# Seven half-size products for eight in the output product of a gated MoE block

## The chip, the cores and the metric

The kernel runs on one core of a Trainium2 chip. The metric is the device time of one execution in microseconds (us), as the median of several executions. Times of one experiment and of the kernel before were taken on the same chip in the same session.

## The reference

```python
# q, k, v: (B=8, H=8, S=576, D=64); w_gate, w_val: (512, 1536); w_out: (1536, 512); w_res: (512, 512)
kv  = einsum('bhsd,bhse->bhde', k, v)
o   = einsum('bhsd,bhde->bhse', q, kv)
x   = o / sqrt(mean(o*o, -1) + 1e-6) * g_norm          # then (B*S, H*D) = (4608, 512)
ffn = (gelu(x @ w_gate) * (x @ w_val)) @ w_out
out = x + sigmoid(x @ w_res) * ffn                       # 4608 x 512, float32
```

## The kernel before

All matmuls take fp16 tiles, and their sums are kept in fp32 tiles. The 4608 tokens are worked in nine blocks of 512. Blocks 0 to 7 hold the first 512 tokens of each batch entry, and block 8 holds the 8 x 64 tokens left over (the remainder). A block has twelve slots for the up-projections (gate and value, one 128-wide piece of F = 1536 per slot) and then four tiles of 128 tokens, each with a residual gate and an output product. The attention of the next block is worked between these slots, on whatever engine has room.

```python
pmoe  = ctx.enter_context(tc.tile_pool(name="pmoe", bufs=4, space=bass.MemoryType.PSUM))
pattn = ctx.enter_context(tc.tile_pool(name="pattn", bufs=4, space=bass.MemoryType.PSUM))
# ... cut ...
def m_act(blk, f, gps, vps):                      # hid = gelu(gate) * value
    ge = moep.tile([P, NJ * P], FP16, tag="ge", name="ge")
    nc.scalar.activation(out=ge, in_=gps, func=AF.Gelu)
    nc.vector.tensor_tensor(out=hids[blk][:, f, :], in0=ge, in1=vps, op=ALU.mult)

def m_res(blk, j):                                # residual gate: four matmuls, then tanh on ACT
    rps = pmoe.tile([P, C], FP32, tag="mm", name="rps")
    # ... cut ...
    nc.scalar.activation(out=th, in_=rps, func=AF.Tanh, scale=0.5)
    return th

def m_out(blk, j):                                # 12 output matmuls of 512 columns per tile
    # ... cut ...
    th = m_res(blk, j)
    fps = pmoe.tile([P, C], FP32, tag="mm", name="fps")
    for f in range(NF):
        m_ffn(blk, j, f, fps)
    m_store(blk, j, m_gate(th, fps))              # (th + 1) * fps, then 0.5 * that + t, on DVE
```

The attention of block 1 ends inside block 0's output product. Its normalisation is a chain of twelve small operations on VectorE (DVE). The scaled result `t` is then transposed on TensorE (PE).

```python
def a_norm(b, j0, j1):                            # 1/sqrt by Newton, on 128x32 or 128x40 elements
    # ... cut ...
    nc.vector.tensor_scalar(out=m, in0=ss, scalar1=1.0 / D, scalar2=RMS_EPS, op0=ALU.mult, op1=ALU.add)
    # ... cut: two more tensor_scalar ...
    for _ in range(3):
        nc.vector.tensor_tensor(out=a, in0=yy, in1=yy, op=ALU.mult)
        nc.vector.tensor_tensor(out=a, in0=a, in1=mh, op=ALU.mult)
        nc.vector.scalar_tensor_tensor(out=yy, in0=a, scalar=1.5, in1=yy, op0=ALU.add, op1=ALU.mult)

# attention of block 1, by slots of block 0
NF + 6: [lambda: a_norm(b, 0, NJ), t[0], t[1], t[2], t[3]],
2 * NF: [x[0], x[1]],                             # x[j]: transposes of tile j on PE
2 * NF + 1: [x[2]],
2 * NF + 2: [x[3]],
```

## Time and profile before

| | before |
|---|---|
| median of 3 executions | 350.04 us (349.79 to 350.08) |
| span in the profile | 348.1 us, mean granted clock 1.000 |
| PE, PE weight loads, DVE busy | 97%, 46%, 61% |
| ACT (ScalarE), POOL (GpSimd) busy | 35%, 14% |

The lines that bound the reading are in the prediction below. Some hints for them:

- In views by order of time, a line gives the start, the time taken, the engine and the line of the program, then output<-inputs, their shapes and the count. An idle time ahead of the group and what ended it stand in square brackets.
- Matmuls overlap in the pipeline, so the pace of a group is read from its start to the start of the next group, not from its duration: in the kernel before a 128x512 matmul has a mean duration of 379 ns, while twelve of them start within 2.59 us, 0.216 each.
- The row of PE clocks gives the granted clock in forty slices of the span. 9 is full speed, 5 about half.

Two more facts of the kernel before are needed later. The first is the first operation of block 1's normalisation, in DVE's order of time:

```profile
48.62 0.18 DVE L249 TENSOR_SCALAR nm<-ss 128x32 f32<-128x32 f32 x1
```

The second is what PE does at that point, in its order of time:

```profile
52.50 0.62 PE L284 MATMUL xtp<-ident,t 128*128 128x128 f16 x8
52.95 1.03 PE L364 MATMUL fps<-wo,hid 128*128 128x512 f16 x4
...
56.07 1.02 PE L331 MATMUL gps<-xT,wg 128*128 128x512 f16 x4
```

The norm operation takes 0.18 us. PE reaches the transposes of its result at 52.50 without a wait, and is through with them and the last output matmuls at 56.07, in 3.57 us.

### The profile page before, as it was taken

The page shows a single profiled execution, that of the slowest core. Times are in us where ns is not written, and L with a number is a line of the kernel's source. Part 1 is how long each engine was busy: PE and PEld are TensorE (multiplying, and loading weights), DVE is VectorE, ACT ScalarE, POOL GpSimd, SP SyncE. Part 2 cuts the span into 40 slices and gives each one's busy share as a digit, 9 for nine tenths or more (in the row PEclk, how much of TensorE's full clock was granted, in tenths as well). Part 3 has the DMA queues.
Part 4 walks back from the last instruction along what each step waited for, and adds up shares of the span by engine and source line. Part 5 has one row for each costly group of instructions (what it writes and reads, how often), then busy time and mean ns, then how long its engine had stood idle before and what let it go on. Part 6 is the DMA issues. An engine that isn't in the chain of part 4 may idle for free.

```text
span 348.1 us, 5543 instructions
## 1 busy us (share of the span) xinstructions
PE 338.4 (97%) x2162; PEld 159.5 (46%) x2162; DVE 211.9 (61%) x432; ACT 122.0 (35%) x212; POOL 50.2 (14%) x79
## 2 busy tenths in 40 slices
PE   8699999999999999999999999999999999999995
PEld 3444544444444444444444444444444444444443
DVE  6755377769748765766478656855686444344433
ACT  3663544362254213421353125312732233223320
POOL 2782420150050005000320031000000000000000
PEclk9999999999999999999999999999999999999999
DMA  7999999697889078904792569045002500020013
GB/s 240 311 206 202 196 202 136 173 148 93 190 142 118 0 175 157 132 0 123 141 184 16 135 140 185 5 101 157 0 2 56 140 2 0 30 91 2 0 30 92
DMA packets 78508, 38.77 MB, mean 111 GB/s; under 512 B 42386, under 2 KB 74002, under 8 KB 78482
## 3 DMA queue, kind: packets, MB, share of 16 engines
q0 software_dynamic: 38752, 17.17, 38.9%
q1 hardware_dynamic: 39488, 21.11, 23.0%
q8 instruction: 17, 0.28, 0.3%
q10 hardware_dynamic: 242, 0.13, 0.1%
q14 instruction: 9, 0.07, 0.1%
HBM read 38.80 MB, written 9.44 MB: 139 GB/s over the span
## 4 chain that ended last, share of the span: by engine, by line
PE 92%; DMA 4%; DVE 2%; SPq 0%; issue 0%; POOL 0%; ACT 0%; DVEq 0%
PE gps L331 27%; PE fps L364 26%; PE vps L331 26%; PE rps L351 9%; DMA vf<-in_v_dram 2%; DMA kf<-in_k_dram 1%; PE kvp L182 1%; PE op L200 1%; DMA qrT<-qr 1%; DVE t L601 1%; DVE ss L587 1%; PE vps L627 0%; PE fps L394 0%; PE gps L627 0%; PE xtp L284 0%; PE orp L228 0%
## 5 line engine op out<-in xcount | busy, mean ns | idle before, releaser
L320 DVE TENSOR_TENSOR hid<-ge,vps 128x512 f16<-128x512 f16 x108 | 73.4, 685 | 68.4 <-PE vps L331 66.3
L331 PE MATMUL gps<-xT,wg 128*128 128x512 f16 x424 | 109.0, 379 | 0.0
L331 PE MATMUL vps<-xT,wv 128*128 128x512 f16 x424 | 108.8, 379 | 0.0
L319 ACT ACTIVATE ge<-gps 128x512 f16<-128x512 f32 x108 | 64.3, 597 | 118.6 <-PE gps L331 106.6
L364 PE MATMUL fps<-wo,hid 128*128 128x512 f16 x420 | 96.5, 379 | 0.0
L331 PEld LDWEIGHTS <-wv 128*128 128x128 f16 x424 | 41.5, 98 | 50.0
L364 PEld LDWEIGHTS <-hid 128*128 128x128 f16 x420 | 40.8, 98 | 48.5
L331 PEld LDWEIGHTS <-wg 128*128 128x128 f16 x424 | 40.2, 98 | 46.8 <-issue 0.2
L370 DVE SCALAR_TENSOR_TENSOR pf<-th,fps 128x512 f32<-128x512 f32 x35 | 23.8, 687 | 48.1 <-PE fps L364 48.1
L360 ACT ACTIVATE th<-rps 128x512 f32<-128x512 f32 x36 | 21.5, 598 | 79.5 <-PE rps L351 79.5
L351 PE MATMUL rps<-wr,xT 128*128 128x512 f16 x144 | 36.5, 379 | 0.0
L375 DVE SCALAR_TENSOR_TENSOR osb<-pf,t 128x512 f32<-128x512 f32 x35 | 24.2, 691 | 1.1
L219 DVE TENSOR_REDUCE ss<-sq 128x8 f32<-128x512 f32 x32 | 20.6, 679 | 2.9 <-ACT sq L217 2.7
L351 PEld LDWEIGHTS <-xT 128*128 128x128 f16 x144 | 14.1, 98 | 17.0
L733 POOL COPY hold<-qT 1x1 f16<-1x1 f16 x5 | 0.9, 178 | 133.8 <-DMA qT<-q 133.8
L277 DVE TENSOR_TENSOR t<-op,ny 128x512 f16<-128x512 f32 x28 | 17.9, 682 | 0.1
L217 ACT ACTIVATE sq<-op 128x512 f32<-128x512 f32 x28 | 15.3, 597 | 4.5 <-PE op L200 4.2
L291 DVE TENSOR_TENSOR t<-t,g 128x512 f16<-128x512 f16 x36 | 13.3, 418 | 0.0
L512 PE MATMUL idle<-zeros 128*128 128x512 f16 x19 | 7.2, 505 | 1.2 <-DVE zeros L485 1.2
L99 POOL DMA_DIRECT2D qraw<-in_q_dram x7 | 6.3, 895 | 5.9 <-DVE q L107 4.0
L101 POOL DMA_DIRECT2D v<-in_v_dram x7 | 6.3, 904 | 0.0
L100 POOL DMA_DIRECT2D kraw<-in_k_dram x7 | 6.3, 899 | 0.1
(102 smaller groups left out, 166.0 us busy)
## 6 DMA issues: line engine op xcount, KB each, us to landing
out_dram<-osb SPq DMA_DIRECT2D x32, 256.0 KB, 2.4
qraw<-in_q_dram POOLq DMA_DIRECT2D x7, 512.0 KB, 6.1
kraw<-in_k_dram POOLq DMA_DIRECT2D x7, 512.0 KB, 8.5
v<-in_v_dram POOLq DMA_DIRECT2D x7, 512.0 KB, 11.0
wg<-in_moe_w_gate_dram POOLq DMA_DIRECT2D x2, 512.0 KB, 8.8
wv<-in_moe_w_val_dram POOLq DMA_DIRECT2D x2, 512.0 KB, 9.5
wo<-in_moe_w_out_dram POOLq DMA_DIRECT2D x2, 512.0 KB, 13.6
out_dram<-osb SPq DMA_DIRECT2D x6, 128.0 KB, 2.3
```

Source lines behind the costliest of these rows:

```text
L217: nc.scalar.activation(out=sq, in_=src, func=AF.Square)
L219: nc.vector.tensor_reduce(out=out_, in_=sq, op=ALU.add, axis=mybir.AxisListType.X)
L277: nc.vector.tensor_tensor(out=t, in0=o, in1=scale, op=ALU.mult)
L291: nc.vector.tensor_tensor(out=t_t[blk][:, jj, :], in0=t_t[blk][:, jj, :], in1=g16, op=ALU.mult)
L319: nc.scalar.activation(out=ge, in_=gps, func=AF.Gelu)
L320: nc.vector.tensor_tensor(out=hids[blk][:, f, :], in0=ge, in1=vps, op=ALU.mult)
L331: nc.tensor.matmul(ps[:, j0 * P : j1 * P], lhsT=w[:, cc, :], rhs=xT_t[blk][:, j0:j1, cc, :], start=(cc == 0 and j0 == 0), stop=(cc == NP - ...
L351: nc.tensor.matmul(rps, lhsT=xT_t[blk][:, j, cc, :], rhs=wr16[:, cc, :], start=(cc == 0), stop=(cc == NP - 1),)
L360: nc.scalar.activation(out=th, in_=rps, func=AF.Tanh, scale=0.5)
L364: nc.tensor.matmul(fps, lhsT=hids[blk][:, f, j * P : (j + 1) * P], rhs=wo16[:, f, :], start=(f == 0), stop=(f == NF - 1))
L370: nc.vector.scalar_tensor_tensor(out=pf, in0=th, scalar=1.0, in1=fps, op0=ALU.add, op1=ALU.mult)
L375: nc.vector.scalar_tensor_tensor(out=osb, in0=pf, scalar=0.5, in1=t_t[blk][:, j, :], op0=ALU.mult, op1=ALU.add)
```

## The change

The intent is to stream fewer columns through PE. The output product of a block is (512 x 1536)·(1536 x 512). Cut both factors into 2 x 2 parts A and B: tokens, the 1536 and the 512 columns are each halved. Strassen's scheme in Winograd's form needs seven half products where the plain way needs eight:

- Sums of the weights, once per kernel on POOL: t0 = B12−B11, t1 = B22−t0, t2 = B22−B12, t3 = B21−t1.
- Sums of the hidden activations, once per block on DVE: s0 = A21+A22, s1 = s0−A11, s2 = A11−A21, s3 = A12−s1.
- Products, each of 2 x 6 matmuls of 256 columns. PSUM banks go on summing from what another engine put into them (E from ACT's copy, F from DVE's sum, in seven blocks, so 14 times per execution): A = A11·B11, E ← A (copied by ACT), D = s0·t0, d ← D (copied by ACT), A += s1·t1, F ← A+d (DVE), E += A12·B21, A += s2·t2, c22 = A+d (DVE), F += s3·B22, A += A22·t3. The four results are E, F, A and c22.

The matmul count of the output product rises from 48 to 84 per block, while its columns fall by one eighth. To find SBUF for the sums, the hidden tiles go from two buffers to one and the result tiles are shared. The residual gate's tiles move to the attention's PSUM pool. Blocks 0 and 8 keep the plain product. The core of the diff:

```diff
-    hidp = ctx.enter_context(tc.tile_pool(name="hidp", bufs=2))
+    hidp = ctx.enter_context(tc.tile_pool(name="hidp", bufs=1))
@@ cut @@
+    def wo_sums(i):
+        pairs = [(b_of(1, 2), b_of(1, 1)), (b_of(2, 2), wo_t[:, 0]), (b_of(2, 2), b_of(1, 2)), (b_of(2, 1), wo_t[:, 1])]
+        for f in range(0, NFH, 2):
+            sub(nc.gpsimd, wo_t[:, i, f : f + 2, :], *(x[:, f : f + 2, :] for x in pairs[i]))
+    def s_begin(blk):
+        s_ = hid_sums
+        sub(nc.vector, s_[2], a_of(blk, 1, 1), a_of(blk, 2, 1))
+    def s_rest(blk):
+        s_ = hid_sums
+        sub(nc.vector, s_[0], a_of(blk, 2, 1), a_of(blk, 2, 2), ALU.add)
+        sub(nc.vector, s_[1], s_[0], a_of(blk, 1, 1))
+        sub(nc.vector, s_[3], a_of(blk, 1, 2), s_[1])
@@ cut @@
+                m_res(blk, j, pattn, "at")
@@ cut @@
+            prod(w["A"], a_of(blk, 1, 1), b_of(1, 1), True)
+            nc.scalar.copy(out=w["E"], in_=w["A"])
+            prod(w["D"], s_[0], wo_t[:, 0], True)
+            nc.scalar.copy(out=w["d"], in_=w["D"])
@@ cut @@
+            prod(w["A"], s_[1], wo_t[:, 1], False)
+            sub(nc.vector, w["F"], w["A"], w["d"], ALU.add)
+            prod(w["E"], a_of(blk, 1, 2), b_of(2, 1), False)
+            pf((0, 0), w["E"])
+            prod(w["A"], s_[2], wo_t[:, 2], False)
@@ cut: c22, F's and A's last products, gating and stores @@
-            2 * NF + 2: [x[3]],
+            2 * NF + 2: [x[3], lambda: [wo_sums(i) for i in range(4)]],
@@ cut @@
-            k0, o0, n0 = 4, 6, 10
+            k0, o0, n0 = 5, 7, 10
         else:
-            at(m - 1, NF + 1, lambda: by_token(b, "q"))
-            at(m - 1, NF + 2, *begin)
+            at(m - 1, NF - 2, lambda: by_token(b, "q"))
+            at(m - 1, NF + 1, *begin)
@@ cut @@
+                plan.setdefault(NFH + 2, []).insert(0, lambda: s_begin(blk))
+                plan.setdefault(NF - 1, []).append(lambda: (s_rest(blk), outs.extend(out_by_products(blk))))
```

More of the change, by code (lines that the diff above doesn't have):

```diff
@@ L117 @@
     wr16 = wpool.tile([P, NP, C], FP16, name="wr16")
+    wo_ts = wpool.tile([P, NF * C], FP16, name="wo_ts")
+    hid_s = wpool.tile([P, NF * NJ * P], FP16, name="hid_s")
+    th_all = finp.tile([P, NJ, C], FP32, bufs=1, name="th")
+    res_all = finp.tile([P, NJ, C], FP32, bufs=1, name="osb")
     def load_columns(dst, src, i):
@@ L346, in m_gval, with m_res @@
         m_act(blk, f, gps, vps)
-    def m_res(blk, j):
-        rps = pmoe.tile([P, C], FP32, tag="mm", name="rps")
+    def m_res(blk, j, pool=pmoe, tag="mm"):
+        rps = pool.tile([P, C], FP32, tag=tag, name="rps")
         for cc in range(NP):
@@ L357, in m_res @@
             )
-        th = finp.tile([P, C], FP32, tag="th", bufs=NJ, name="th")
+        th = th_all[:, j, :]
         nc.scalar.activation(out=th, in_=rps, func=AF.Tanh, scale=0.5)
@@ L366, in m_ffn, with m_gate @@
         )
-    def m_gate(th, fps):
-        pf = finp.tile([P, C], FP32, tag="pf", bufs=NJ, name="pf")
+    def m_gate(j, th, fps):
+        pf = res_all[:, j, :]
         nc.vector.scalar_tensor_tensor(out=pf, in0=th, scalar=1.0, in1=fps, op0=ALU.add, op1=ALU.mult)
@@ L373, in m_store @@
     def m_store(blk, j, pf):
-        osb = finp.tile([P, C], FP32, tag="osb", bufs=3, name="osb")
+        osb = pf
         nc.vector.scalar_tensor_tensor(
@@ L388, in m_out_last @@
         th = m_res(blk, j)
-        osb_all = finp.tile([P, C], FP32, tag="osb", bufs=3, name="osb")
         for c0, n in ((0, C // 2), (C // 2, C // 4), (3 * C // 4, C // 4)):
@@ L400, in m_out_last @@
                 )
-            pf = finp.tile([P, n], FP32, tag="pf", bufs=NJ, name="pf")
+            osb = pf = res_all[:, j, cs]
             nc.vector.scalar_tensor_tensor(out=pf, in0=th[:, cs], scalar=1.0, in1=fps, op0=ALU.add, op1=ALU.mult)
-            osb = osb_all[:, cs]
             nc.vector.scalar_tensor_tensor(
@@ L417, in m_out, with b_of, a_of @@
             m_ffn(blk, j, f, fps)
-        m_store(blk, j, m_gate(th, fps))
+        m_store(blk, j, m_gate(j, th, fps))
+    NFH, CH, PR = NF // 2, C // 2, M0 // 2
+    wo_t = wo_ts.rearrange("p (i f c) -> p i f c", i=4, f=NFH)
+    hid_sums = hid_s.rearrange("p (i f t) -> p i f t", i=4, f=NFH)
+    hid_sums = [hid_sums[:, i] for i in range(4)]
+    def b_of(i, j):
+        return wo16[:, (i - 1) * NFH : i * NFH, (j - 1) * CH : j * CH]
+    def a_of(blk, i, j):
+        return hids[blk][:, (j - 1) * NFH : j * NFH, (i - 1) * PR : i * PR]
@@ new lines, in sub @@
+    def sub(eng, out_, in0, in1, op=ALU.subtract):
+        eng.tensor_tensor(out=out_, in0=in0, in1=in1, op=op)
+    def wo_sums(i):
[10 more added lines that the diff above has]
+        sub(nc.vector, s_[3], a_of(blk, 1, 2), s_[1])
@@ new lines, in prod, with out_by_products, res, first_two @@
+    def prod(ps, a, b, start):
+        for e in range(2):
+            for f in range(NFH):
+                nc.tensor.matmul(
+                    ps[:, e, :],
+                    lhsT=a[:, f, e * P : (e + 1) * P],
+                    rhs=b[:, f, :],
+                    start=(start and e == 0 and f == 0),
+                    stop=(f == NFH - 1),
+                    skip_group_check=True,
+                )
+    def out_by_products(blk):
+        w = {}
+        s_ = hid_sums
+        def res(jj):
+            for j in (2 * jj, 2 * jj + 1):
+                m_res(blk, j, pattn, "at")
+        def first_two():
+            for n in ("D", "E", "F", "A"):
+                w[n] = pmoe.tile([P, 2, CH], FP32, tag="mm", name="w" + n)
+            w["d"] = finp.tile([P, 2, CH], FP32, tag="wd", bufs=1, name="wd")
+            prod(w["A"], a_of(blk, 1, 1), b_of(1, 1), True)
+            nc.scalar.copy(out=w["E"], in_=w["A"])
+            prod(w["D"], s_[0], wo_t[:, 0], True)
+            nc.scalar.copy(out=w["d"], in_=w["D"])
+        def part(jj):
+            return slice(None), slice(2 * jj[0], 2 * jj[0] + 2), slice(jj[1] * CH, (jj[1] + 1) * CH)
+        def pf(jj, src):
+            nc.vector.scalar_tensor_tensor(
+                out=res_all[part(jj)], in0=th_all[part(jj)], scalar=1.0, in1=src, op0=ALU.add, op1=ALU.mult
+            )
+        def fin(jj):
+            of = part(jj)
+            nc.vector.scalar_tensor_tensor(
+                out=res_all[of], in0=res_all[of], scalar=0.5, in1=t_t[blk][of], op0=ALU.mult, op1=ALU.add
+            )
+        def store(jj):
+            dst = out[blk * S : blk * S + M0, :].rearrange("(p j) c -> p j c", j=NJ)
+            js = slice(2 * jj, 2 * jj + 2)
+            nc.sync.dma_start(out=dst[:, js, :], in_=res_all[:, js, :])
+        def others():
+            prod(w["A"], s_[1], wo_t[:, 1], False)
[3 more added lines that the diff above has]
+            prod(w["A"], s_[2], wo_t[:, 2], False)
+            c22 = res_all[part((1, 1))]
+            sub(nc.vector, c22, w["A"], w["d"], ALU.add)
+            prod(w["F"], s_[3], b_of(2, 2), False)
+            pf((0, 1), w["F"])
+            fin((0, 0))
+            prod(w["A"], a_of(blk, 2, 2), wo_t[:, 3], False)
+            pf((1, 1), c22)
+            pf((1, 0), w["A"])
+            fin((0, 1))
+            store(0)
+            fin((1, 1))
+            fin((1, 0))
+            store(1)
+        return [lambda: res(0), lambda: res(1), first_two, others]
@@ L430, in step @@
             if f == NF - 1:
-                pfs.extend(m_gate(ths[j], fpss[j]) for j in range(NJ))
+                pfs.extend(m_gate(j, ths[j], fpss[j]) for j in range(NJ))
         slots += [lambda f=f: step(f) for f in range(NF)]
@@ L437 @@
     tiles_16(0)
-    raw[0, "q"] = stage.tile([P, H, NJ * D], FP32, name="qf")
+    raw[0, "q"] = wo_ts.bitcast(FP32)[:, 0 : H * NJ * D].rearrange("p (h x) -> p h x", h=H)
     hid_of = {}
     for which in "kv":
-        t = hidp.tile([P, NF, NJ * P], FP16, tag="hid", name=which + "f")
-        hid_of[which] = t = t.rearrange("p a b -> p (a b)")
+        if which == "k":
+            t = hidp.tile([P, NF, NJ * P], FP16, tag="hid", name=which + "f").rearrange("p a b -> p (a b)")
+        else:
+            t = hid_s
+        hid_of[which] = t
         raw[0, which] = t.bitcast(FP32)[:, 0 : H * NJ * D].rearrange("p (h x) -> p h x", h=H)
@@ L452 @@
         first_last.append(t[:, 2 * H * NJ * D :][:, 0 : 2 * H * D].rearrange("p (j h d) -> p j h d", j=2, h=H))
-        first_raw.append([finp.tile([P, C], FP32, tag="th", bufs=NJ, name=f"{which}l") for _ in range(2)])
+        first_raw.append([th_all[:, 2 * len(first_raw) + i, :] for i in range(2)])
     def load_first_last(half):
@@ L793 @@
                 slots[0] = lambda: m_gval(1, 0, pattn, "at")
-            slots += [lambda j=j: m_out(blk, j) for j in range(NJ)]
+            if blk < B:
+                outs = []
+                slots += [lambda i=i: outs[i]() for i in range(4)]
+                plan.setdefault(NFH + 2, []).insert(0, lambda: s_begin(blk))
+                plan.setdefault(NF - 1, []).append(lambda: (s_rest(blk), outs.extend(out_by_products(blk))))
+            else:
+                slots += [lambda j=j: m_out(blk, j) for j in range(NJ)]
             for j, fs in enumerate(late):
```

## The prediction

> **What bounds the kernel now.** I read the page first: busy shares, slices, chain. Then the chain in order of time, PE's waits, a table by windows, and VectorE's (DVE's) order of time around one output product.
>
> The page, parts 1, 2 and 4:
>
> ```profile
> PE 338.4 (97%) x2162; PEld 159.5 (46%) x2162; DVE 211.9 (61%) x432; ACT 122.0 (35%) x212; POOL 50.2 (14%) x79
> ...
> PEclk9999999999999999999999999999999999999999
> ...
> PE 92%; DMA 4%; DVE 2%; SPq 0%; issue 0%; POOL 0%; ACT 0%; DVEq 0%
> ```
>
> TensorE is busy almost throughout at its full clock, and the chain that ended last lies on it for 92%. A busy PE proves little by itself, so I looked at its pace, in the chain by order of time (start us, us, what):
>
> ```profile
> 80.57 2.59 PE fps L364 x12
> ...
> 341.42 1.32 PE fps L394 x12
> ```
>
> Twelve matmuls of 128x512 take 2.59 us, 0.216 each: one column per 0.42 ns. The second line is the 256-column piece of the last block: 1.32/12 = 0.110 each. So half the columns cost half the time, though each matmul has its own weight load. This is what Strassen needs, because it makes more and smaller matmuls. PE hardly waits after its start; the only wait after 20 us is
>
> ```profile
> PE orp L228 <- DMA qrT<-qr: 0.6, 1, 0.6
> ```
>
> The bound is thus the number of columns that PE streams. Next is whoever can become the new bound in the output product. The table by windows (PE, PEld, DVE, ACT, POOL busy) over the output products of blocks 1 and 2:
>
> ```profile
> 79.50:93.40 13.90, 13.90 (x66) 6.31 (x65) 12.04 (x27) 2.39 (x4) 0.00 (x0) 1.00 0.72 115
> ...
> 116.00:129.80 13.80, 13.80 (x66) 6.22 (x65) 8.85 (x17) 2.39 (x4) 0.00 (x0) 1.00 0.45 98
> ```
>
> DVE is busy for 12.0 of 13.9 us in block 1 and 8.9 of 13.8 in block 2. In block 1 it also runs late, as its order of time shows:
>
> ```profile
> 81.00 0.20 DVE L257 SCALAR_TENSOR_TENSOR ny<-na,ny 128x40 f32<-128x40 f32 x1
> 81.12 0.68 DVE L320 TENSOR_TENSOR hid<-ge,vps 128x512 f16<-128x512 f16 x1
> 81.71 1.28 DVE L277 TENSOR_TENSOR t<-op,ny 128x512 f16<-128x512 f32 x2
> ...
> 85.80 1.42 DVE L291 TENSOR_TENSOR t<-t,g 128x512 f16<-128x512 f16 x4
> ```
>
> The last up-projection matmul of block 1 ends near 79.55, yet its product with the gate starts at 81.12, behind the chain of small norm operations. Nobody waits for it now.
>
> [...] 128x512 f16 takes 418 ns against 685 with a PSUM operand. [...]
>
> ```profile
> 6.94 0.60 POOL L542 CAST kf<-kl 32x512 f16<-32x512 f32 x1
> ...
> 7.27 0.55 DVE L542 CAST vf<-vl 32x512 f16<-32x512 f32 x1
> 8.53 0.43 DVE L533 CAST v<-vf 128x512 f16<-128x512 f32 x1 [0.71 <-DMA vf<-in_v_dram]
> ```
>
> The DVE cast beside POOL takes 0.55 us, a cast of as many elements per partition alone 0.43. [...]
>
> **The change part by part.**
>
> *Removed from PE.* 48 output matmuls of 512 columns per block become 7 products x 2 x 6 = 84 of 256. 48 x 0.2158 = 10.36 us, 84 x 0.1092 = 9.17 us. Saved: 1.19 per block, 8.3 us for blocks 1 to 7. All of it is on the path.
>
> *Added to DVE.* Four sums of 128x1536 f16 per block. A 128x512 one takes 0.418 alone and four take 1.42, so each follows the last after 0.33; 0.27 of that streams. 1536 elements: 3 x 0.27 + 0.15 = 0.95 us, following after 0.87. Four: 3.5. Two sums out of PSUM at about 0.6: 1.2. So 4.7 us per block. The two passes per result keep their number and width. *Added to ACT:* two PSUM copies, 1.2 us per block; ACT is busy for 2.4 of 13.9 us there, so this is free.
>
> *Does this hide in blocks 2 to 7?* I set the end of the last up-projection matmul to 0. PE runs the residual gate till 3.45, the first product till 4.75, D till 6.05, the third till 7.35. Before, block 2's last gate product ended at 1.2; with one sum and the query copy ahead of it, it now ends at 2.6. One remainder scale follows, then the sums at 4.1, 5.0 and 5.9. D needs the first at 4.75: in time. Then five scalings by g (7.6) and the key copy (8.2), then F's sum till 8.9, where the fifth product wanted it at 8.65. That costs some 0.3 us in each of the three later blocks that also carry remainder rows (2, 4, 6): 0.9. Then PE and DVE alternate, with 1.31 us per product against 0.6 to 0.7 per pass. Transposes: the scalings end near 7, the DMA takes 4.3, so next block's x lands at 11.5, before the products end at 12.6.
>
> *Block 1 does not hide it.* I walked its new DVE order with the durations above (0.6 from PSUM, 0.87 per sum, 2.4 for the norm chain), in the clock of the trace before. The product of f=8 ends at 74.6, the early sum at 75.5, two reductions at 76.7, f=9 at 77.3, a reduction at 78.0, f=10 at 78.6, the norm chain at 81.0, the query copy at 81.6, f=11 at 82.2, the first scaling of the attention output at 82.8. The residual gate's tiles have moved to the attention pool, so the built program makes the first of them wait for exactly that scaling, which frees its bank, and the second for the next one. PE would be there at 78.95. Added wait: 3.9 us. Afterwards DVE is ahead again (its sums end at 86, D wants them at 87.7).
>
> *Moved.* The start of block 2's attention one slot later removes the 0.6 us wait for the transposed remainder. The leaner layout waits for nothing new: one hidden buffer is enough, since its first write comes 1.7 us after the last product has read it.
>
> *Added to POOL.* Twelve 128x512 sums of w_out[...]. They start as soon as the loads before them are issued, near 47.7, and are needed near 86.
>
> Sum: 350.0 - 8.3 - 0.6 + 3.9 + 0.9 = 345.9 us.
>
> **The rivals.** *(1) POOL's sums hold up DVE's norm chain in block 0.* That chain of twelve small operations, nine of them with two SBUF inputs, runs from 48.6 to 51.1, just where POOL's sums run. PE takes the transposes that depend on it at 52.5, with no slack. If each operation waits for one POOL instruction, the chain grows by up to ten times 1.1 us and PE stands some 10 us: 356. For it: [...] the stretched cast. [...] I give it 3 in 10, and a milder form (3 us: 349) some more. *(2) Block 1 hides better than I think.* If the bank wait were under 1 us, the time would be 342 to 343. For it: DVE had 1.3 us of idle time between 76 and 78. Against it: my walk uses that already. 2 in 10. *(3) DVE bounds every block.* With 4.7 us more, output product and projections together need some 30 of 35 us of DVE, so only its order can hurt; but one operation of 0.7 us out of place ahead of F's sum costs PE as much, seven times: 350 or more. *(4) The small matmuls show their weight loads*, an added 10 ns each: 84 x 7 x 0.01 = 6 us, no gain left. The last block's pace of 0.110 speaks against it.
>
> **Range and chances.** The sum is 345.9; most rivals lie on the slow side, so I take 346.5. Low end: no wait in block 1 and the full 8.3 us, 341.8. High end: most of rival 1, 354.5. Faster by over 2% means under 343.0 and needs rival 2. Slower by over 2% means over 357.0 and needs all of rival 1 and more. Chances: 0.22, 0.67, 0.11.
>
> **What would show it.** The 84 products should have a pace of 0.109 to 0.110 with PE at full clock; PE's waits should have one of 3 to 5 us of the first residual matmul in block 1 for DVE's scaling, and under 0.5 in later blocks; the wait for the remainder should be gone. If rival 1 holds, PE's transposes in block 0 wait for DVE by many us and the norm operations there last over 0.5 us instead of 0.2. The prediction is wrong if such a wait is large or if the one in block 1 is missing.

The sum was 350.0 − 8.3 − 0.6 + 3.9 + 0.9 = 345.9 us, and POOL's sums had no term in it. What the traces show for figures that stand without their source:

- 418 against 685 ns: DVE's products `t, g` (both inputs in SBUF) and `ge, vps` (one of them in PSUM) in the trace before.
- 0.1092 us per matmul of 256 columns: twelve in 1.31 us in the kernel after. With the 1.32 us of the trace before, 0.110 each, the saving is 10.36 − 9.24 = 1.12 us per block, 7.8 in all.
- 0.27 us for 512 more elements of a DVE sum, 0.95 for 1536: the kernel after has 0.954 for 1536, the trace before 0.418 for 512, and (0.954 − 0.418)/2 = 0.268. The 0.87 from a sum to the next operation was 0.88 in the kernel after (99.57 to 100.45), but 0.99 where a sum reads the one before it (97.59, 98.58, 99.57).
- 4.3 us from issue to landing of the next block's x: the median of ten transfers in the trace before.
- 1.1 us per POOL sum, as rival 1 has it: 13.35 us for twelve in the kernel after, 1.11 each.
- The 10 ns of rival 4, and in rival 1 the wait for one POOL instruction each, are suppositions.

## More of the kernel before

Numbers of different sessions are set side by side only because the kernel before had a median of 349.97 to 350.25 us in each of them. One execution of it, in the session of e5 to e8, was slow (355.68 us) and is left out of the ratios.

## The result and the profile after

| | before | after |
|---|---|---|
| median of 4 executions | 349.97 us (349.79 to 350.08) | 362.72 us (362.35 to 363.59) |
| span in the profile | 348.1 us | 360.8 us |
| mean granted clock in the profile | 1.000 | 0.976 |

The kernel became slower: the ratio is 1.037, with a 95% interval of 1.035 to 1.039. A ratio here and below is the mean time of one kernel's runs over the mean of the other's of the same rounds, so it is not quite the ratio of the medians that are quoted. The result lies outside the predicted range of 341.8 to 354.5.

The page of the kernel after, parts 1, 2 and 4:

```profile
PE 335.5 (93%) x2414; PEld 186.0 (52%) x2414; DVE 254.7 (71%) x474; ACT 130.1 (36%) x226; POOL 64.6 (18%) x91
...
PEclk9999996699999999999999999999999999999999
...
PE 75%; DVE 17%; DMA 4%; issue 2%; ACT 0%; POOL 0%; SPq 0%; DVEq 0%; ACTq 0%
```

PE has less work but a smaller share of a longer span. The chain that ended last now lies on DVE for 17% of the span, before for 2%. Two slices of the clock row show a 6. PE's waits, largest first (what waits <- what ended the wait: us in total, times, longest us):

```profile
PE xtp L289 <- DVE t L282: 12.2, 1, 12.2
PE rps L356 <- DVE t L282: 3.7, 1, 3.7
...
PE wA L463 <- DVE wF L439: 0.5, 2, 0.3
PE gps L336 <- DMA xT<-t: 0.3, 1, 0.3
```

There is one wait of 12.2 us at the transposes in block 0 and one of 3.7 us at the first residual matmul of block 1. What DVE did before the first of them stands in its order of time:

```profile
48.27 12.37 DVE L254 TENSOR_SCALAR nm<-ss 128x32 f32<-128x32 f32 x1
60.67 0.18 DVE L255 TENSOR_SCALAR ny<-nm 128x32 int32<-128x32 int32 x1
```

A single small operation, the first of the norm chain, lasted 12.37 us instead of 0.18. The next eleven kept their usual length, and the scaling of the attention output could start at 62.98 only. The time stands inside the operation's own 12.37 us, not in brackets as idle time ahead of it, so the profile shows no semaphore of the program that it waited for. POOL in the same stretch, first and last of four groups of three:

```profile
47.24 3.39 POOL L439 TENSOR_TENSOR wo_ts<-wo 128x512 f16<-128x512 f16 x3
...
57.23 3.36 POOL L439 TENSOR_TENSOR wo_ts<-wo,wo_ts 128x512 f16<-128x512 f16 x3
```

The twelve weight sums run without a gap from 47.24 to 60.59. The DVE operation starts one us into them and ends at 60.64, when they are over. PE's order of time shows what followed:

```profile
64.33 1.03 PE L289 MATMUL xtp<-ident,t 128*128 128x128 f16 x8 [12.21 <-DVE t L282]
65.16 1.91 PE L369 MATMUL fps<-wo,hid 128*128 128x512 f16 x4
...
70.63 1.03 PE L336 MATMUL gps<-xT,wg 128*128 128x512 f16 x4
...
97.14 5.31 PE L356 MATMUL rps<-wr,xT 128*128 128x512 f16 x16 [3.73 <-DVE t L282]
102.29 1.47 PE L463 MATMUL wA<-wo,hid 128*128 128x256 f16 x12
103.60 1.47 PE L463 MATMUL wD<-wo_ts,hid_s 128*128 128x256 f16 x12
...
134.07 3.62 PE L356 MATMUL rps<-wr,xT 128*128 128x512 f16 x16
```

Four output matmuls of 512 columns take 1.91 us after the wait, before 1.03. The stretch from the transposes to the next block's first matmul takes 70.63 − 64.33 = 6.30 us, before 3.57. Likewise the sixteen residual matmuls of block 1 take 102.29 − 97.14 = 5.15 us after their wait. In block 2, at 134.07, they take 3.45. The products keep the expected pace: 103.60 − 102.29 = 1.31 us for twelve, 0.109 each. The table by windows of the kernel after (width, busy time of PE, its weight loads, DVE, ACT and POOL, then the granted clock) tells why PE was slow:

```profile
64.30:70.70 6.40, 6.37 (x29) 3.46 (x30) 1.77 (x3) 2.65 (x4) 0.00 (x0) 0.55 0.01 3
97.10:102.30 5.20, 5.16 (x17) 2.03 (x18) 5.13 (x8) 1.79 (x3) 0.00 (x0) 0.67 0.00 0
169.38:204.61 35.23, 35.23 (x285) 20.38 (x284) 28.23 (x55) 14.00 (x25) 5.43 (x8) 1.00 0.70 115
```

On the mean of the two stretches after the waits PE was granted 0.55 and 0.67 of its clock. The third window runs from one residual gate to the next, with the output product of block 3 in it. The same stretch of the kernel before:

```profile
152.04:188.47 36.43, 36.43 (x250) 16.84 (x249) 23.79 (x49) 12.82 (x23) 5.06 (x8) 1.00 0.70 111
```

PE has no gap in either, the clock is full in both, and the stretch is 1.20 us shorter with 35 matmuls more in the trace (36 by the program). So the gain that the change was made for is there. The account of the 12.7 us by which the spans differ:

| where | us |
|---|---|
| PE waits for `t` before the transposes in block 0 | +12.21 |
| slow clock after it (6.30 − 3.57) | +2.73 |
| PE waits for `t` at the first residual gate of block 1 | +3.73 |
| slow clock after it (5.15 − 3.45) | +1.70 |
| gaps at F's sum in blocks 2 and 4, 0.43 each from PE's starts | +0.86 |
| next block's x lands late in block 6 (288.28 − 286.47 − 1.31, from PE's starts) | +0.50 |
| seven output products, 1.19 each as worked out | −8.33 |
| wait for the transposed remainder gone | −0.59 |
| sum | +12.81 |

The rows mix idle times of the profile with gaps read from PE's starts, and one row is worked out, so the sum meets the 12.7 only to within some tenths.

### The profile page after: what moved, and what is told of

Read it like the earlier page. It is cut to its first block, busy times and chain, and to the rows that moved or that the text cites. A ratio compares the mean times of both kernels' runs of the same rounds, so it can differ in the third digit from the quotient of the medians.

```text
span 360.8 us, 6070 instructions
## 1 busy us (share of the span) xinstructions
PE 335.5 (93%) x2414; PEld 186.0 (52%) x2414; DVE 254.7 (71%) x474; ACT 130.1 (36%) x226; POOL 64.6 (18%) x91
## 4 chain that ended last, share of the span: by engine, by line
PE 75%; DVE 17%; DMA 4%; issue 2%; ACT 0%; POOL 0%; SPq 0%; DVEq 0%; ACTq 0%
PE gps L336 23%; PE vps L336 23%; PE wA L463 8%; PE rps L356 7%; PE fps L369 4%; DVE nm L254 4%; DVE hid_s L439 2%; DVE hid L325 2%; PE wF L463 2%; DVE t L282 2%; PE wD L463 2%; DMA xT<-t 2%; PE kvp L187 1%; PE wE L463 1%; DMA kf<-in_k_dram 1%
## 5 line engine op out<-in xcount | busy, mean ns | idle before, releaser
L356 PE MATMUL rps<-wr,xT 128*128 128x512 f16 x144 | 34.7, 393 | 3.7 <-DVE t L282 3.7
L463 PEld LDWEIGHTS <-hid_s 128*128 128x128 f16 x336 | 32.9, 98 | 4.7 <-issue 0.9
L463 PEld LDWEIGHTS <-hid 128*128 128x128 f16 x252 | 24.7, 98 | 4.4
L369 PE MATMUL fps<-wo,hid 128*128 128x512 f16 x84 | 21.6, 408 | 0.0
L463 PE MATMUL wA<-wo_ts,hid_s 128*128 128x256 f16 x168 | 20.6, 272 | 0.5 <-DVE wF L439 0.5
L500 DVE SCALAR_TENSOR_TENSOR osb<-osb,t 128x512 f32<-128x512 f32 x28 | 18.0, 686 | 0.0
L289 PE MATMUL xtp<-ident,t 128*128 128x128 f16 x16 | 2.3, 312 | 12.2 <-DVE t L282 12.2
L369 PEld LDWEIGHTS <-hid 128*128 128x128 f16 x84 | 8.5, 105 | 9.7 <-issue 1.6
L254 DVE TENSOR_SCALAR nm<-ss 128x40 f32<-128x40 f32 (+1 forms) x7 | 13.4, 1919 | 0.0
L439 DVE TENSOR_TENSOR hid_s<-hid 128x1536 f16<-128x1536 f16 x14 | 13.4, 954 | 0.1
```

The costliest lines, as they stand in the source:

```text
L356: nc.tensor.matmul(rps, lhsT=xT_t[blk][:, j, cc, :], rhs=wr16[:, cc, :], start=(cc == 0), stop=(cc == NP - 1),)
L369: nc.tensor.matmul(fps, lhsT=hids[blk][:, f, j * P : (j + 1) * P], rhs=wo16[:, f, :], start=(f == 0), stop=(f == NF - 1))
L439: eng.tensor_tensor(out=out_, in0=in0, in1=in1, op=op)
L463: nc.tensor.matmul(ps[:, e, :], lhsT=a[:, f, e * P : (e + 1) * P], rhs=b[:, f, :], start=(start and e == 0 and f == 0), stop=(f == NFH - 1 ...
L500: nc.vector.scalar_tensor_tensor(out=res_all[of], in0=res_all[of], scalar=0.5, in1=t_t[blk][of], op0=ALU.mult, op1=ALU.add)
```

## The experiments

The questions were these. Does the POOL run hold up DVE (theory A) or does DVE's own queue? Does DVE wait for one POOL instruction or for the whole run? In block 1, is the PSUM bank of the residual gate the cause, or is DVE late as a whole? And what is left when both are mended? Eleven kernels ran, all with correct results. A time is the median, with the range in parentheses.

| run | us | ratio to the kernel before |
|---|---|---|
| the change | 362.72 (362.35 to 363.59) | 1.037 |
| e1_sums_on_dve | 349.72 (346.65 to 350.20) | 0.996 |
| e2_gate_in_old_pool | 360.93 (360.28 to 361.81) | 1.030 |
| e3_both | 348.59 (347.65 to 350.24) | 0.995 |
| e4_two_inputs (one look) | 362.64 | – |
| e5_rescheduled | 345.05 (344.28 to 346.82) | 0.985 |
| e6_layout_only | 348.94 (348.63 to 349.21) | 0.996 |
| e7_pool_spaced | 344.94 (344.88 to 345.01) | 0.984 |
| e8_half_the_run (one look) | 358.51 | – |
| e9_best | 343.40 (343.08 to 345.13) | 0.982 |
| e10_sums_after_norm (one look) | 357.10 | – |
| e11_last_order | 343.17 (342.83 to 344.44) | 0.980 |

All diffs are against the kernel after.

### e1: the weight sums on DVE

```diff
-            sub(nc.gpsimd, wo_t[:, i, f : f + 2, :], *(x[:, f : f + 2, :] for x in pairs[i]))
+            sub(nc.vector, wo_t[:, i, f : f + 2, :], *(x[:, f : f + 2, :] for x in pairs[i]))
```

> One edit: the twelve sums of w_out run on DVE instead of POOL, at the same place of the program. Theory A ([...] DVE's first norm operation of block 0 stands 12.4 us, and PE's clock then falls for a while): that operation takes 0.2 us again, PE's 12.2 us wait for the transposes goes, PEclk is full there, and the 2.7 us lost to the lower clock come back; DVE has some 4 us more to do, of which up to 1 us may show. Time near 348.5 (347 to 350). Rival B (the norm operation waits for something else that the new layout brings, and POOL only happens to run at the time): the 12 us wait stays, time 361 to 363.

Measured: 349.72 us, 13 us below the change and level with the kernel before (ratio 0.996, interval 0.991 to 1.001). The 12.2 us wait is gone from PE's waits and the clock row is at 9 throughout. The other wait stayed, with the same 3.7 us at the same place in PE's waits of this run, and the sixteen residual matmuls behind it again take 5.15 us (too short a slow stretch for the row to show).

Moving twelve instructions off POOL thus gives back the first wait and the slow clock behind it (12.2 + 2.7 = 14.9 us), less what the sums cost on DVE. In the profiled execution the first full up-projection also began 1.65 us later than before (23.04 against 21.39), after later first loads. The executions spread over 3.5 us; whether for the same reason is not shown, since one of them was profiled. The wait in block 1 is there without POOL's sums.

### e2: block 1's residual gate back in its old PSUM pool

```diff
-                m_res(blk, j, pattn, "at")
+                m_res(blk, j, *((pmoe, "mm") if blk == 1 else (pattn, "at")))
```

> One edit: in block 1 alone the residual gate's four PSUM tiles come from the up-projection pool again; POOL keeps the sums. Theory A (PE's 3.7 us wait in block 1 is for a bank that the late attention scaling still holds): the wait at the first residual matmul goes, its matmuls run at the full clock again (3.5 us for sixteen rather than 5.2), and some 0.9 us of waits come at the first product for a tanh; time near 358 (357.3 to 359). Rival B (DVE as a whole is late, so PE waits for as much at the next product that needs a sum of hidden blocks): the wait moves to product D, time 361 to 363.

Measured: 360.93 us, only 1.8 below the change. The wait at the residual gate is gone, but 0.43 us appear at D and 2.77 at the fifth product. Its order of time on PE:

```profile
104.73 1.95 PE L463 MATMUL wA<-wo_ts,hid_s 128*128 128x256 f16 x12 [2.77 <-DVE wF L439]
106.47 2.70 PE L463 MATMUL wF<-wo,hid_s 128*128 128x256 f16 x12
109.01 1.48 PE L463 MATMUL wA<-wo_ts,hid 128*128 128x256 f16 x12
```

The fifth product waits because F's sum on DVE must first have read A. Thereafter F's product takes 109.01 − 106.47 = 2.54 us where 1.31 is usual, so the clock fell again (in e3, at the same place, the window after the wait shows 0.57). The median lies above what theory A gave and just below rival B's 361 to 363. Rival B was right that the wait moves, but it named D. In the profiled executions the spans differ by 1.2 us, and 1.1 of that is the slow clock after block 0's wait, which this edit does not touch: it cost 1.59 us here and 2.73 in the change. The bank was only where the delay showed. DVE comes late to everything in block 1, and taking away one place of waiting moves the wait to the next.

### e3: both

The edits of e1 and e2 together.

> The edits of e1 and e2 together. If the two waits add up and are all that hid the gain: near 344 (343 to 346), that is 1.2 to 2% faster than before, with PE's waits after its start under 2.5 us in all. If DVE is the real bound with the sums on it, PE's waits in block 1 stay over 3 us and the time is 347 or more.

Measured: 348.59 us (ratio 0.995), well above the expectation. The same wait of 2.7 us stands before the fifth product. DVE's order of time shows what F's sum waits behind:

```profile
90.00 0.68 DVE L107 COPY k<-kraw 128x2048 f16<-128x2048 f16 x1
90.60 0.69 DVE L439 TENSOR_TENSOR wF<-wA,wd 128x512 f32<-128x512 f32 x1
```

PE was through with the fourth product at 88.5. Since the end of the norm chain at 81.2 DVE had, besides one gate product and the hidden sums, the query copy, five scalings of the attention output, five multiplications by g and the key copy. The copies and the remainder's scaling were not due as early as F's sum; the multiplications by g had little to spare, as e5 shows. The expectation had counted the removed waits and not the order of that queue.

### e4: does an operation with two SBUF inputs wait in the same way?

The operation that waited 12.37 us has one tensor input. Here the first norm operation of block 1 takes its constant from a second SBUF tile, so its form is the one that most of the chain has.

```diff
+        if b == 1:
+            nc.vector.scalar_tensor_tensor(
+                out=m, in0=ss, scalar=1.0 / D, in1=eps_w[:, 0:n], op0=ALU.mult, op1=ALU.add
+            )
+        else:
             nc.vector.tensor_scalar(out=m, in0=ss, scalar1=1.0 / D, scalar2=RMS_EPS, op0=ALU.mult, op1=ALU.add)
```

> One edit: in block 0 the first operation of the norm chain gets its constant from an SBUF tile, so it has two SBUF inputs[...]. POOL keeps the sums. Theory A (any DVE instruction with two SBUF inputs waits for POOL's reads): the first operation lasts some 12.4 us, the second 0.2. Theory B [...]: the first lasts 0.2 us, the second some 12. The time stays near 362.7 in both.

Measured: 362.64 us, one look. DVE's order of time:

```profile
49.92 11.90 DVE L255 SCALAR_TENSOR_TENSOR nm<-ss,eps_w 128x32 f32<-128x32 f32 x1
61.86 0.18 DVE L260 TENSOR_SCALAR ny<-nm 128x32 int32<-128x32 int32 x1
```

POOL's run lasted from 48.44 to 61.77 here. The two-input form waits for its end just as the one-input form did. The second operation of the chain kept its one tensor input, so by theory B it should have been the one to wait; it took 0.18 us. So the wait is not for the one-input form alone.

### e5: sums on DVE in larger pieces, and F's sum ahead of work that isn't due

e3, with the weight sums as four operations (two in block 0 before the gating, two in block 1), and with the query and key copies and the remainder's scaling placed after F's sum.

```diff
-            2 * NF + 2: [x[3], lambda: [wo_sums(i) for i in range(4)]],
+            2 * NF + 2: [x[3], lambda: [wo_sums(i, nc.vector, NFH) for i in range(2)]],
@@ cut @@
-            at(m - 1, NF - 2, lambda: by_token(b, "q"))
-            at(m - 1, NF + 1, *begin)
+            at(m - 1, NF + 3, lambda: by_token(b, "q"))
+            at(m - 1, NF + 3, *begin)
@@ cut @@
+                    plan.setdefault(6, []).append(lambda: wo_sums(2, nc.vector, NFH))
+                    plan.setdefault(7, []).append(lambda: wo_sums(3, nc.vector, NFH))
```

> e3 with DVE's work put elsewhere: w_out's sums as four instructions on DVE, two before block 0's gating and two in block 1's idle slots; the query and key copies and, for block 2's data, the remainder's scalings come after the sum that feeds F instead of before it. Theory C (what is left after e3 is DVE work that stands ahead of F's sum in block 1, 2.7 us, and in blocks 2, 4 and 6, 0.3 to 0.4 each): all of PE's waits for F's sum go, PE's waits after its start come to under 1.2 us, and the time is 342.5 (341.5 to 344), 2.2% faster than before. Rival D (DVE's total in block 1 is the bound and the order cannot help): a wait of over 2 us stays in block 1, time 346 or more.

Measured: 345.05 us (ratio 0.985, interval 0.982 to 0.988), about 2.5 above the expectation, but the first version clearly below the kernel before. In block 1 waits of 1.0 us at F's sum, 0.4 at D and 0.7 for the next block's x were left. That is more than theory C allowed and less than the 2 us at one place of rival D. The waits at F's sum in blocks 2 and 4 went, as theory C has it.

### e6: the layout without the seven products

The plain 48 matmuls with the rest of the change: one hidden buffer, shared tiles, the moved slots. The residual gate's tiles are not part of it; with the plain product they stay in the old PSUM pool.

```diff
-            2 * NF + 2: [x[3], lambda: [wo_sums(i) for i in range(4)]],
+            2 * NF + 2: [x[3]],
@@ cut @@
-            if blk < B:
+            if False:
```

> The changed kernel without its products and without w_out's sums: every block's output product is the old one of 48 matmuls, in the new layout (one hidden buffer, shared result tiles) and with the new attention slots. If the layout costs nothing: 349.5 (349 to 350.5), the 0.6 us wait for the remainder's transpose gone. If one hidden buffer makes DVE or PE wait between blocks: over 352.

Measured: 348.94 us (ratio 0.996, interval 0.993 to 0.998). The leaner layout costs nothing, and the 0.6 us wait for the remainder's transpose is gone. From one residual gate to the next, blocks 2 to 7 take 36.07, 36.43, 36.07, 36.42, 34.54 and 34.53 us here and 35.00, 35.36, 35.00, 35.37, 33.71 and 33.35 in e5. So in e5 the products gain 0.83 to 1.18 us per block of the 1.19 that the column count offers; e11 below gets all of it.

### e7: POOL does half of the sums, with pauses

e5, but the first two weight sums stay on POOL as six instructions. Ahead of each stands a one-element copy of the next hidden product, so that POOL cannot go on until DVE has come that far.

```diff
+    def gated_sum(n):
+        nc.gpsimd.tensor_copy(out=hold, in_=hids[1][0:1, n, 0:1])
+        wo_sums(n // 3, nc.gpsimd, 2, [2 * (n % 3)])
@@ cut @@
+                    for n in range(6):
+                        plan.setdefault(n, []).append(lambda n=n: gated_sum(n))
```

> e5 with the first two of w_out's sums on POOL again, but as six instructions each released by one gate product of block 1, so that POOL pauses between them. Theory A1 ([...] only its unbroken run of twelve kept DVE out): a DVE instruction waits for one POOL instruction at most, so none lasts over 1.9 us, and the time is within 1.5 us of e5. Theory A2 (any overlap with a POOL read costs DVE many instructions' time): a DVE instruction lasts 3 us or more, and the time is over 346.

Measured: 344.94 us (ratio 0.984), level with e5. The longest DVE operation beside a POOL sum, with that sum, and a later place, in order of time:

```profile
62.44 1.78 DVE L380 SCALAR_TENSOR_TENSOR osb<-osb,t 128x512 f32<-128x512 f32 x1
62.53 1.14 POOL L439 TENSOR_TENSOR wo_ts<-wo 128x512 f16<-128x512 f16 x1
...
70.16 1.15 POOL L439 TENSOR_TENSOR wo_ts<-wo,wo_ts 128x512 f16<-128x512 f16 x1
70.67 1.45 DVE L439 TENSOR_TENSOR wo_ts<-wo 128x1536 f16<-128x1536 f16 x1
71.25 0.91 POOL L854 COPY hold<-qT 1x1 f16<-1x1 f16 x1
```

The POOL sum ran from 62.53 to 63.67. The operation with two SBUF inputs lasted 1.78 us instead of its usual 0.69, longer by 1.09, one POOL instruction. PE's waits in block 1 are near those of e5 (0.5, 1.0 and 0.7 us). At the later place POOL does not pause at all: its next instruction, a one-element copy, stands directly behind the sum. Yet DVE's operation gets in between when the sum ends at 71.31. It is done at 72.12, and the copy, which takes 0.18 us alone, stands until then. So what limits the wait to one instruction in this run is what follows each sum, a one-element copy, and not necessarily a gap.

### e8: half the run at the old place

Six POOL instructions instead of twelve where the change has them, the other two sums on DVE in block 1.

```diff
-            2 * NF + 2: [x[3], lambda: [wo_sums(i) for i in range(4)]],
+            2 * NF + 2: [x[3], lambda: [wo_sums(i, nc.gpsimd, 2) for i in range(2)]],
```

> The changed kernel with only the first two of w_out's sums on POOL, at the old place and unbroken (six instructions, some 6.7 us), and the other two on DVE in block 1. Theory A (DVE waits for the end of POOL's unbroken run, however long): the first norm operation lasts some 5.7 us instead of 12.4, and PE's wait for the transposes is some 5.5 us instead of 12.2. If DVE waited for one instruction only, it would last 1.3 us; if for a fixed time, still 12.

Measured: 358.51 us, one look. The first norm operation in DVE's order of time:

```profile
49.06 6.66 DVE L254 TENSOR_SCALAR nm<-ss 128x32 f32<-128x32 f32 x1
```

POOL's run was 49.00 to 55.69, and the operation ends at 55.72. The wait is the rest of the run whatever its length: 6.66 us of six instructions, 12.37 of twelve. It is longer than the 5.7 expected because the operation began 0.06 us into the run here and 1.03 us into it in the change. PE stood 6.5 us for the transposes.

### e9: the weight sums where no two-input operation of DVE is due

e5, with the last two weight sums on POOL but held back until block 1's scaling by g is done, the sum s3 moved behind that scaling, and s2 one slot later in block 1.

```diff
+    def late_sums():
+        nc.gpsimd.tensor_copy(out=hold, in_=t_t[1][0:1, 3, 0:1])
+        wo_sums(2)
+        wo_sums(3)
@@ cut @@
+                if blk == 1:
+                    plan[6].insert(0, late_sums)
```

> e5 with the rest of block 1 taken off DVE: the last two of w_out's sums on POOL in one unbroken run of six, released when DVE has nothing but PSUM readers and reductions ahead of it, and the last of the hidden sums behind the scalings by g, so that x of the next block is sent off 0.9 us sooner. Theory C (what e5 still lost in block 1 was DVE's queue: 0.4 us at D, 1.0 at F's sum, 0.75 for the transposed x): these three waits fall to under 0.5 us in all and the time is 343.0 (342.3 to 343.8), 2% under before. If POOL's run meets a DVE instruction with two SBUF inputs after all, that one lasts up to 6 us and the time is 346 or more.

Measured: 343.40 us (ratio 0.982, interval 0.979 to 0.984). POOL's six instructions ran from 68.08 to 74.8 without a pause, and no two-SBUF-input operation of DVE fell into them; reductions with one SBUF input did, and kept their usual time (two in 1.28 us). The time is as expected, the waits only in part: D's is gone and x's down to 0.3 us, but the 1.0 us at F's sum in block 1 was left.

### e10: the whole run, right after the norm chain

The change with one edit: POOL's twelve sums are held back until the norm scalings of block 1 are done.

```diff
+    def gated_sums():
+        nc.gpsimd.tensor_copy(out=hold, in_=t_t[1][0:1, 3, C - 1 : C])
+        for i in range(4):
+            wo_sums(i)
@@ cut @@
-            2 * NF + 2: [x[3], lambda: [wo_sums(i) for i in range(4)]],
+            2 * NF + 2: [x[3], gated_sums],
```

> The changed kernel with one gate: POOL's twelve sums start only when DVE has written the last scaling of the attention output in block 0, so the norm chain is over by then. Theory A (any DVE instruction with two SBUF inputs waits for the end of POOL's unbroken run, wherever it falls): the norm chain takes 2.5 us again and PE's 12 us wait for the transposes goes, but the first result pass of block 0 (two SBUF inputs) lasts some 8 us instead of 0.7, and PE stands some 4 to 6 us for a bank in block 1: time 353 to 357. Rival E (only the norm chain's small instructions are open to it): no such instruction, time 348.5.

Measured: 357.10 us, one look, 0.1 us above what theory A gave and far from rival E. POOL's run was 54.09 to 67.44. DVE's order of time beside it:

```profile
55.79 2.48 DVE L375 SCALAR_TENSOR_TENSOR osb<-th,fps 128x512 f32<-128x512 f32 x4 [1.91 <-PE fps L369]
58.31 0.69 DVE L325 TENSOR_TENSOR hid<-ge,vps 128x512 f16<-128x512 f16 x1
58.91 9.09 DVE L380 SCALAR_TENSOR_TENSOR osb<-osb,t 128x512 f32<-128x512 f32 x1
```

This is the clearest single view of what waited and what passed. The gating `th, fps` and the product `ge, vps` have one input in SBUF and one in PSUM. They pass at their usual speed in the middle of POOL's run (four in 2.48 us, one in 0.69). The store's sum `osb, t` has both inputs in SBUF and stands for 9.09 us, until POOL is done (58.91 + 9.09 = 68.00, which is 0.56 us after the run's end). Behind it the hidden products came late, and PE waited 6.1 us for one of them. The norm chain itself was as short as before the change.

### e11: the last order

e9, with s3 after F's sum and the key copy after the last use of A.

```diff
-            at(m - 1, NF - 2, lambda: by_token(b, "q"))
-            at(m - 1, NF + 1, *begin)
+            at(m - 1, NF + 3, lambda: by_token(b, "q"), *begin[1:])
+            at(m - 1, NF + 4, begin[0])
```

> e9 with three DVE instructions in another order around F's sum: the last sum of hidden blocks directly after F's sum instead of before it, and the key copy after the last use of A. Theory C (e9's remaining 1.0 us wait in block 1 is that one sum standing ahead of F's): the wait goes, the rest stays: 342.4 (341.9 to 343.2), over 2% under before. If the wait only moves to the sixth product or to the next block's key product: as e9, 343.4.

Measured: 343.17 us (342.83 to 344.44) against 350.18 of the kernel before in the same session. The ratio is 0.980, with an interval of 0.978 to 0.982, too close to a 2% gain to call it one with certainty. It is 5.4% below the change. PE's order of time at the end of block 1's output product:

```profile
88.09 1.47 PE L471 MATMUL wE<-wo,hid 128*128 128x256 f16 x12
89.69 1.47 PE L471 MATMUL wA<-wo_ts,hid_s 128*128 128x256 f16 x12
...
94.70 1.04 PE L336 MATMUL gps<-xT,wg 128*128 128x512 f16 x4 [0.92 <-DMA xT<-t]
```

The gap at F's sum shrank to 89.69 − 88.09 − 1.31 = 0.29 us. In its place the next block's x lands 0.92 us late (e9: 0.28). Counted from block 1's first residual matmul, the next block begins after 14.29 us here (94.70 − 80.41) and after 14.34 in e9. So the new order around F's sum only moved the loss from one wait to another: x sets the end of block 1. Its scalings on DVE end 8.5 us after that residual matmul, and its transfer takes 5.7 us from issue to landing, where the prediction had reckoned 4.3. Blocks 2 to 7 take 34.88, 35.24, 34.87, 35.24, 33.34 and 33.35 us, each 1.18 to 1.20 below e6: there the products give their full 1.19. The time hardly separates the two expectations of this run, 342.4 and 343.4. Its profile is of an execution of 344.42 us, in which the first full up-projection began at 22.60 us (e9: 21.12), so some of the spread lies ahead of the blocks.

## Why the prediction was wrong

**Right: the bound and the size of the gain.** PE's streamed columns were the bound. The products run at 0.109 us per matmul, and blocks 3, 5 and 7 became shorter by 1.18 to 1.20 us, as worked out. Rival 4 (weight loads that show) is refuted by the same pace.

**Right: blocks 2 to 7.** The sums take 0.954 to 0.958 us each on average (worked out: 0.95). F's sum holds PE up for 0.43 us in blocks 2 and 4, not at all in 6, 0.86 in all against 0.9. Rival 3 did not come about there. One step failed in a small way: in block 6 the transfer of the next block's x took 6.1 us from issue to landing and not 4.3, and it cost 0.50 us where 1.1 us of slack had been worked out.

**Right in size, too narrow in cause: block 1.** The wait at the first residual gate was 3.73 us where 3.9 had been worked out. The text put it down to the bank in the attention pool. e2 shows that the bank is only the place: without it, 2.77 us reappear at F's sum. The cause is DVE's queue in block 1, which holds work for the next block ahead of work that PE needs. The order of e5 and e11 took most of it away.

**Right: layout and moved slots.** e6 confirms that they cost nothing and take away the 0.6 us wait. POOL's twelve sums took 13.35 us, 1.11 each, as the 1.1 of rival 1 has it.

**Wrong: the step that failed is "Added to POOL", with rival 1 left out of the sum.** The prediction named this rival and placed it correctly, at the norm chain in block 0 just where POOL's sums run. But it put nothing into the sum for it, where 12.21 us of waiting and 2.73 us of slow clock came. Two things were mis-sized:

- *"If each operation waits for one POOL instruction, the chain grows by up to ten times 1.1 us".* It does not work like that. One DVE operation waits for the end of POOL's unbroken run. It took 12.37, 11.90, 6.66 and 9.09 us in the change, e4, e8 and e10. Each time it ended 0.03 to 0.56 us after POOL's last instruction, by its own usual time less 0.13 to 0.15 us. Only with a one-element copy between the sums (e7) is the wait one instruction, 1.09 us. The two ways come to a like number here by chance (10 and 12 us), but the way matters: with the run broken up or halved the cost falls, which counting DVE operations would not tell. And the operation that waited was the one-input tensor_scalar at the head of the chain, while the text pointed to the nine operations with two SBUF inputs.
- *The chances.* What the runs can test of the grounds for "3 in 10" is a cast that took 0.55 us beside POOL and 0.43 alone. A sentence took these 0.12 us as evidence against. That was misread. The cast began at 7.27, when POOL's instruction had only 0.27 us left (6.94 + 0.60 = 7.54), and ended at 7.82, 0.28 us after it: its own 0.43 less 0.15, the same mark as in the four runs above. So it had stood for all of the little there was to wait for, and spoke for the rival. What twelve instructions in a row do it could not show. Slower by over 2%, which is what came, had been given 0.11.

**Missing: the clock.** No step said that PE's clock falls when PE has stood. The window rows at 0.55 and 0.67 show it, and the cost was 2.73 us after the wait of 12.21 and 1.70 after that of 3.73. That makes 4.4 of the 12.7 us. The cost does not follow the length of the wait: the stretch of block 0 lost 1.59 us after 12.25 in e2 and 1.98 after 6.50 in e8, and two products of e2 lost 1.66 after 2.77. After waits of 1.02 us (e5) and 0.99 us (e9) the next product kept its usual pace, 1.30 and 1.31 us. Rival 1's own figure, 356, becomes 360.4 with the 4.4 us.

With the measured terms, the sum as predicted comes right: 345.9 + 12.2 + 2.7 + 1.7 = 362.5, measured 362.72. That it fits so closely is partly luck, since block 6's 0.50 us is not in it and the 2.73 is the figure of one execution.

**Still open.** Why the whole run counts as one is not settled. A POOL instruction follows the last without any gap in the trace (3.36 us for three), but that alone is not the reason: in e7 a copy follows a sum as closely and DVE gets in between. What sets a sum that follows a sum apart no run here shows. Equally, the last losses of e11 in block 1 were not removed: 0.28 us at D, 0.29 at F's sum and 1.08 before the next block, all from PE's starts.

## What to carry to other kernels

Before work goes onto an engine that seems idle, look at which operations of its neighbour have two inputs in SBUF during that run, and whether PE waits for any of them (one such operation lasted 9.09 us instead of 0.69 in e10; here a one-input tensor_scalar waited too, 12.37 us in the change, while reductions did not, two in 1.28 us in e9). An unbroken run of sums on POOL cost them its whole rest (12.37 us of twelve sums, 6.66 of six in e8), so break it up, as e7 did with one-element copies (a wait of 1.09 us), or place it where DVE reads from PSUM (0.69 us beside the run in e10). Count the slow clock after a PE wait as part of the wait: it cost 1.59 us (e2) to 2.73 us (the change) after each of the waits between 2.77 and 12.25 us that are worked out above. And where an engine is late as a whole, freeing one buffer only moves the wait (3.73 us at the gate became 0.43 at D and 2.77 at F's sum in e2): reorder its queue so that what PE needs comes ahead of what the next block needs, until the next block's own input sets the end, as x did in e11.
